# Loading the first weight matrix of a decode step in two transfers, 16 rows and 112 rows

## The chip, the core and the metric

One Trainium2 chip, one of its cores. The metric is the device time of one execution in microseconds; the figure of the kernel before is the median of three runs, 1299.67 us (1299.64 to 1299.94 us). Profiles show one execution each, and their time is compared with the median below.

## The reference

A decode step of two sequences with one token each (B = 2, D = 512): the normalized token attends over a key and value cache of 32 heads with 8192 positions of 128 numbers each, the attention's output goes through `wo`, and it is multiplied by a gate that a small MLP computes from the same token. Everything is float32.

```python
xn = layernorm(x)
q  = (xn @ wq) split in 32 heads of 128
s  = softmax(q . k_cache / sqrt(128)) . v_cache  @ wo      # k_cache, v_cache: 2 x 32 x 8192 x 128
g  = silu(gelu(layernorm(xn) @ w1 + b1) @ w2 + b2)         # w1: 512 x 1376, w2: 1376 x 512
out = x + s * g
```

The caches are 256 MB each (2 x 32 x 8192 x 128 numbers of 4 bytes, in MB of 2^20 bytes); the weights `w1`, `w2`, `wq` and `wo` are some 22 MB together.

## The kernel before, in words

The 64 pairs of sequence and head are handled two at a time, in 32 units. A unit's keys are 128 partitions with 64 KB each, 8 MB, and so are its values. Two buffers `kb` take the keys in turn, one buffer `vb` takes the values. For each unit VectorE multiplies the keys by the query (L550) and sums over the head's 128 numbers (L557), the maximum goes over TensorE (L564, L573), ScalarE takes exponentials (L578), and TensorE multiplies them with the values (L601).

Before the first unit a prologue computes the query and the gate. Its weights lie in the buffers of the main loop, which are still free then: `wq` in `kb[0]`, and `w1`, `w2`, `x`, `b1`, `b2` and all small work tiles side by side in `vb` (L281 ff., hence a profile names them all `vb`). The prologue runs: layernorm of x (L391 to L396), transposes (L403), x times `w1` (L439, with the bias in L441), gelu, times `w2` (L481), the gate (L488 to L497), the query (L510, L515, L521, L522). At the end `wo` is loaded into `vb` in five pieces and multiplied (L674, L683), the gate is applied (L691, L692), and the result is stored (L693).

All transfers are issued by one queue, SyncE's (SP), through the helper `load` (L325), in the order of the program; each has a semaphore of its own. The prologue's order is

```python
    load(w1_sb, w1.rearrange("(p c) f -> p c f", p=P), "w1", ["w1"])
    load(x_sb, x.rearrange("b s d -> (b s) d"), "x", ["x"])
    load(w2_sb, w2.rearrange("f n -> (f n)").rearrange("(p e) -> p e", p=P), "w2", ["w2"])
```

and after it `b1`, `b2`, `wq`, the first unit's keys in two halves (L357), the second unit's keys (`load_k(1)`, L527) and the first unit's values (`load_v(0)`, L533). The second unit's keys go into `kb[0]` and so wait until L510 has read `wq` from it; the first values go into `vb` and so wait until the prologue has read all that lies there. From then on each load waits only for the reads of what its buffer held.

A row of `w1` here is what one partition gets: four rows of the matrix in a piece, 4 x 1376 numbers, 22,016 bytes without a gap in memory. The class `Plan` collects every operation with what it reads and writes (the keys in the lists) and puts in the semaphore waits; the order on each engine is that of the program.

Of the kernel before, what the change touches and what calls it, by code (L numbers as in the profile page):

```python
# [20 lines left out]
class Plan:  # L21
# [18 lines left out]
    def op(self, eng, fn, r=(), w=(), over=(), it=None, loop=False, dma=None):  # L40


        o = Op()
        o.eng, o.fn, o.it, o.loop, o.dma, o.tell = eng, fn, it, loop, dma, False
        need = {}

        def after(d, war):
            if d.dma is None and dma is None and d.eng == eng and (eng == "pe" or war):
                return
            if d.dma is None:  # L50
                if need.get(d.eng) is None or need[d.eng].idx < d.idx:
                    need[d.eng] = d
            else:
                k = ("dma", d.dma)
                if need.get(k) is None or need[k].idx < d.idx:
                    need[k] = d

        for k in r:
            if k in self.writer:
                after(self.writer[k], False)  # L60
        for k in list(w) + list(over):
            if k in self.writer:
                after(self.writer[k], False)
            for d in self.readers.get(k, ()):
                after(d, True)
        clock = self.clock[eng]
        need = {k: d for k, d in need.items() if clock.get(k, 0) < d.idx}
        o.deps = [(k, d) for k, d in need.items()
                  if not any(e is not d and e.done.get(k, 0) >= d.idx for e in need.values())]
        for _, d in o.deps:  # L70
            for k, v in d.done.items():
                clock[k] = max(clock.get(k, 0), v)
        own = eng if dma is None else ("dma", dma)
        self.count[own] = o.idx = self.count.get(own, 0) + 1
        o.done = dict(clock)
        o.done[own] = o.idx
        for k in w:
            self.writer[k] = o
            self.readers[k] = []
        for k in r:  # L80
            if k not in w:
                self.readers.setdefault(k, []).append(o)
        self.ops.append(o)
# [91 lines left out]
def decode_kernel(nc, x, kc, vc, wq, wo, w1, b1, w2, b2, out):  # L175
    P = 128
# [32 lines left out]
    def pe(fn, r=(), w=(), it=None, loop=False):  # L209
        op("pe", fn, r, w, it=it, loop=loop)  # L210

    def dve(fn, r=(), w=(), it=None, loop=False):
        op("dve", fn, r, w, it=it, loop=loop)

    def act(fn, r=(), w=(), it=None, loop=False):
        op("act", fn, r, w, it=it, loop=loop)
# [55 lines left out]
    def take(name, p, n, base=0, at=None):  # L272

        if at is None:
            at = used[0]
            used[0] += n
            assert used[0] <= KP * DH
        boot.append(name)
        return vb[base:base + p, at:at + n]

    w1_sb = take("w1", P, ND * F).rearrange("p (c f) -> p c f", f=F)  # L281
# [18 lines left out]
    yT = take("yT", P, ND * B).rearrange("p (c b) -> p c b", b=B)  # L300
# [13 lines left out]
    def bank():  # L314
        i = turn[0] % 4
        turn[0] += 1
        return scratch[i], f"s{i}"
# [6 lines left out]
    def load(dst, src, sem, w, over=(), it=None):  # L324
        op("sp", lambda *i: nc.sync.dma_start(dst, src(*i) if callable(src) else src), (), w, over=over,  # L325
           it=it, loop=it is not None, dma=sem)
# [21 lines left out]
    WIDE = WO_PIECES[-4]  # L348


    load(w1_sb, w1.rearrange("(p c) f -> p c f", p=P), "w1", ["w1"])
    load(x_sb, x.rearrange("b s d -> (b s) d"), "x", ["x"])
    load(w2_sb, w2.rearrange("f n -> (f n)").rearrange("(p e) -> p e", p=P), "w2", ["w2"])
    for t, src, k in ((b1_sb, b1, "b1"), (b2_sb, b2, "b2")):
# [55 lines left out]
    for j in range(QT):  # L410
        pe(lambda j=j: matmul(px[R * j:R * j + RM, :P], pick, x_sb[:, j * P:(j + 1) * P],
                              start=True, stop=True), ["pick", "x"], [kx])
# [19 lines left out]
    def mlp():  # L432

        chunks = range(0, F, 512)
        for f in chunks:
            w = min(512, F - f)
            ph, k = bank()
            for c in range(ND):
                pe(lambda f=f, w=w, ph=ph, c=c: matmul(ph[:B, :w], yT[:, c, :], w1_sb[:, c, f:f + w],  # L439
                                                       start=(c == 0), stop=False), ["yT", "w1"], [k])  # L440
            pe(lambda f=f, w=w, ph=ph: matmul(ph[:B, :w], ones[R:R + 1, :B], b1_sb[:, f:f + w],  # L441
                                              start=False, stop=True), ["ones", "b1"], [k])
            act(lambda f=f, w=w, ph=ph: nc.scalar.copy(h_nat[:, 1 + f:1 + f + w], ph[:B, :w]),  # L443
                [k, "h_nat"], [("h_nat", f)])

        for m in range(QT):
            dve(lambda m=m: nc.vector.tensor_copy(  # L447
                h_row[:, :, m::QT],
                h_nat[:, WM * m:WM * m + WB * R].rearrange("b (k e) -> b e k", e=WB)[:, :WR, :]),
                ["h_nat"] + [("h_nat", f) for f in chunks], [("h_row", m)])  # L450
        ph, k = bank()
        for r in range(WR):
            pe(lambda r=r: transpose(ph[:, r * B:(r + 1) * B], h_row[:, r, :], ident[2 * R:2 * R + B, 2 * R:2 * R + B]),
               ["ident"] + [("h_row", m) for m in range(QT)], [k])

        act(lambda: nc.scalar.copy(h, ph[:, :WR * B].rearrange("p (r b) -> p r b", b=B)), [k], ["h"])
        dve(lambda: nc.vector.tensor_mul(u, h, h), ["h"], ["u"])
        dve(lambda: nc.vector.tensor_scalar(u, u, GELU_A, 1.0, op0=ALU.mult, op1=ALU.add), ["u"], ["u"])
        dve(lambda: nc.vector.tensor_mul(u, u, h), ["u", "h"], ["u"])
        act(lambda: nc.scalar.activation(u, u, AF.Tanh, scale=GELU_C), ["u"], ["u"])  # L460
        dve(lambda: nc.vector.scalar_tensor_tensor(u, u, 1.0, h, op0=ALU.add, op1=ALU.mult), ["u", "h"], ["u"])
        dve(lambda: nc.vector.tensor_scalar_mul(u, u, 0.5), ["u"], ["u"])

        parts = []
        for c in range(QT):
            for lo, hi, r, m in ((0, c + 1, 1, QT - 1 - c), (c + 1, QT, 0, 0)):
                if lo == hi:
                    continue
                parts.append(("hs", c, lo))

                def part(c=c, lo=lo, hi=hi, r=r, m=m):
                    shape = [P, WM, hi - lo, B]
                    return nc.vector.tensor_tensor(
                        out=hs[:, :, c, lo:hi, :], in0=u[:, r:r + WM, :].unsqueeze(2).to_broadcast(shape),
                        in1=cls[:, m:m + hi - lo].unsqueeze(1).unsqueeze(3).to_broadcast(shape), op=ALU.mult)
                dve(part, ["u"] + [("cls", m) for m in range(QT)], [parts[-1]])
        pw, kw = bank()
        for a in range(WM):
            j = a % QT
            w = min(512, WB * P - a * 512)  # L480
            pe(lambda a=a, j=j, w=w: matmul(pw[R * j:R * (j + 1), :w], hs[:, a].rearrange("p c j b -> p (c j b)"),  # L481
                                            w2_sb[:, a * 512:a * 512 + w], start=(a < QT), stop=(a + QT >= WM)),
               parts + ["w2"], [kw])
        act(lambda: nc.scalar.copy(g_sb, pw), [kw], ["g"])

        p, kp = bank()
        for c in range(QT):
            pe(lambda c=c: matmul(p[:, :P], fold[:, c, :], g_sb[:, c * P:(c + 1) * P], start=(c == 0), stop=False),  # L488
               ["fold", "g"], [kp])
        for j in range(QT):  # L490
            pe(lambda j=j: matmul(p[R * j:R * j + RM, :P], ones[R:R + 1, :], b2_sb[:, j * P:(j + 1) * P],
                                  start=False, stop=True), ["ones", "b2"], [kp])

        act(lambda: nc.scalar.copy(z, p[:, :P]), [kp], ["z"])
        act(lambda: nc.scalar.activation(th, z, AF.Tanh, scale=0.5), ["z"], ["th"])
        dve(lambda: nc.vector.scalar_tensor_tensor(th, th, 1.0, z, op0=ALU.add, op1=ALU.mult), ["th", "z"], ["th"])
        dve(lambda: nc.vector.tensor_scalar_mul(gate, th, 0.5), ["th"], ["gate"])  # L497

    mlp()

    for i in range(NQ):
        for c in range(ND):
            wv = wq_sb[:, c, :].rearrange("p (h s d) -> p h s d", s=U, d=DH)
            a = (NQ - 1 - i) * B
            for j in range(QT):
# [4 lines left out]
                    start=(i + c == 0), stop=(i == NQ - 1 and c == ND - 1)),  # L513
                   ["xnT"] + [("kb", 0, s) for s in range(2)], ["po"])
    act(lambda: nc.scalar.copy(q_nat, PO), ["po"], ["o4"])  # L515
    for k in range(N // NB):

        b, e = divmod(k, HH // NB)
        i, g = divmod(e, GQ)
        p, kp = bank()  # L520
# [147 lines left out]
    def piece(c):  # L668
        return ("wo", max(i for i, a in enumerate(WO_PIECES[:-1]) if a <= c))


    for c in range(WIDE):
        j = c % QT
        pe(lambda c=c, j=j: matmul(wide[R * j:R * j + RM, :], on[:, :, c], wo_sb[:, c, :],  # L674
                                   start=(c < QT), stop=(c + QT >= WIDE)), ["on", piece(c)], ["wide"])
# [47 lines left out]
```

## Time and profile before

| | |
|---|---|
| median of three runs | 1299.67 us (1299.64 to 1299.94) |
| the profiled execution's time | 1299.52 us |
| its span, first to last instruction | 1298.2 us |
| VectorE busy | 1134.3 us, 87% |
| TensorE busy | 408.3 us, 31% |
| ScalarE busy | 77.7 us, 6% |
| moved by DMA | 559.42 MB, mean 431 GB/s |
| w1 and w2, 2752 KB each | 9.3 and 15.0 us from issue to landing |
| mean granted TensorE clock | 0.629 |

A profile is read by its parts: busy time by engine, the span in 40 slices, the DMA queues, the chain of waits that ended last, and the groups of instructions. An engine's share of the span says little by itself; what counts is which wait ends last in each stage. "DMA share" is the mean share of time in which the core's 16 DMA engines were occupied by packets; since a packet is counted where it begins, short stretches show shares over 1. In the chain, a line that begins with DMA is time spent waiting for that transfer to land.

### The profile page before, as it was taken

The numbers are of one execution on the slowest core, as the hardware profiler recorded it, in microseconds if no ns is written. First come the engines' busy times: TensorE is split into PE (matmuls) and PEld (weight loads), VectorE is DVE, ScalarE is ACT, GpSimd is POOL, SyncE is SP. The second block draws the span as 40 slices with busy tenths as digits, with TensorE's granted clock in tenths as the row PEclk, the third lists the DMA queues.
The fourth block names the chain that finished last, engine by engine and source line by source line (L and its number), as shares of the span: only waits on it lengthen the run. The fifth ranks groups of instructions, "written<-read, shape, count | busy, mean of one in ns | idle before, by whom it ended". The sixth has DMA issues, their size and how long they took to land.

```text
span 1298.2 us, 6929 instructions
## 1 busy us (share of the span) xinstructions
PE 408.3 (31%) x2712; PEld 124.1 (10%) x2712; DVE 1134.3 (87%) x276; ACT 77.7 (6%) x250; POOL 2.6 (0%) x10
## 2 busy tenths in 40 slices
PE   5602333312333311333321333321333321333337
PEld 1200111000101000101100101100101100001102
DVE  2499999888889988889988888988888988888991
ACT  1200000000000000000000000000000000000000
POOL 0000000000000000000000000000000000000000
PEclk9856666556666556666555666655666655666659
DMA  9999999999999999999999999999999999999998
GB/s 404 447 422 445 428 420 446 426 444 428 436 432 424 446 426 442 428 426 444 424 446 426 436 432 424 446 426 442 428 428 442 424 446 426 438 430 424 433 434 363
DMA packets 10940, 559.42 MB, mean 431 GB/s; under 512 B 1220, under 2 KB 1332, under 8 KB 1592
## 3 DMA queue, kind: packets, MB, share of 16 engines
q1 hardware_dynamic: 10936, 559.36, 99.7%
q8 instruction: 3, 0.05, 0.0%
q14 instruction: 1, 0.01, 0.0%
HBM read 559.30 MB, written 0.06 MB: 431 GB/s over the span
## 4 chain that ended last, share of the span: by engine, by line
DMA 70%; PE 25%; DVE 3%; issue 1%; ACT 0%; SPq 0%; DVEq 0%
DMA vb<-in_A_v_cache_dram 67%; PE po L601 22%; DMA vb<-in_A_wo_dram 2%; DVE kb L550 1%; DVE sc L557 1%; PE s L439 1%; DMA vb<-in_A_x_dram 1%; PE po L510 1%; PE s L481 0%; PE s L441 0%; PE acc L683 0%; SPq L325 0%; DVE vb L447 0%; ACT L460 0%; PE s L488 0%
## 5 line engine op out<-in xcount | busy, mean ns | idle before, releaser
L550 DVE TENSOR_TENSOR kb<-kb,Q 128x8192 f32<-128x8192 f32 x64 | 555.5, 8681 | 102.7 <-DMA kb<-in_A_k_cache_dram 93.8
L557 DVE TENSOR_REDUCE sc<-kb 128x64 f32<-128x8192 f32 x64 | 552.3, 8666 | 0.0
L601 PE MATMUL po<-vb,PZ 128*8 128x512 f32 x1984 | 286.4, 742 | 288.2 <-DMA vb<-in_A_v_cache_dram 286.9
L573 PE MATMUL s<-nm,srow 1*128 1x2 f32 x64 | 18.4, 355 | 361.5 <-DVE nm L567 361.5
L601 PEld LDWEIGHTS po<-vb,PZ 128*8 128x8 f32 x1984 | 57.1, 104 | 491.3 <-issue 490.0
L564 PE MATMUL s<-ident,mx 128*1 128x128 f32 x32 | 11.8, 369 | 191.7 <-DVE mx L561 191.7
L573 PEld LDWEIGHTS s<-nm,srow 1*128 1x128 f32 x64 | 15.7, 303 | 370.8 <-DVE nm L567 370.8
L608 ACT COPY o<-po 128x512 f32<-128x512 f32 x32 | 18.7, 585 | 533.7 <-PE po L601 533.7
L574 ACT COPY bias<-s 128x2 f32<-128x2 f32 x32 | 5.1, 160 | 618.3 <-PE s L573 618.3
L610 PE MATMUL s<-mod,o 128*128 128x2 f32 x256 | 33.6, 253 | 22.1 <-ACT o L608 22.1
L610 PEld LDWEIGHTS s<-mod,o 128*128 128x128 f32 x256 | 31.0, 191 | 51.3 <-ACT o L608 51.3
L578 ACT ACTIVATE PZ<-sc,bias 64x128 f32<-64x128 f32 x64 | 25.5, 399 | 1.8
L564 PEld LDWEIGHTS s<-ident,mx 128*1 128x1 f32 x32 | 2.5, 79 | 195.1 <-DVE mx L561 164.7
L616 DVE TENSOR_TENSOR Z<-blk,s 128x8 f32 (+1 forms) x32 | 5.2, 163 | 12.4 <-PE s L610 12.4
L447 DVE COPY vb<-vb 2x384 f32<-2x384 f32 x4 | 1.8, 501 | 14.8 <-ACT vb L443 14.8
L578 ACT ACTIVATION_READ_ACCUMULATOR PZ<-sc,bias 64x1 f32 x64 | 11.8, 185 | 0.0
L691 DVE TENSOR_TENSOR gate<-acc,gate 128x128 f32<-128x128 f32 x1 | 0.3, 292 | 13.2 <-PE acc L683 13.2
L439 PE MATMUL s<-vb 128*2 128x512 f32 (+1 forms) x24 | 11.4, 623 | 0.3 <-ACT vb L404 0.3
L561 DVE TENSOR_REDUCE mx<-sc 128x1 f32<-128x128 f32 x32 | 9.2, 286 | 1.1
L582 ACT ACTIVATE ZR<-half,rs 128x8 f32 (+1 forms) x32 | 9.6, 301 | 4.1
L601 PE MATMUL po<-kb,PZ 128*8 128x512 f32 x64 | 8.8, 710 | 1.4 <-ACT PZ L578 1.4
L567 DVE TENSOR_REDUCE nm<-s 1x2 f32<-1x128 f32 x32 | 8.7, 272 | 0.3 <-PE s L564 0.3
(89 smaller groups left out, 84.3 us busy)
## 6 DMA issues: line engine op xcount, KB each, us to landing
kb<-in_A_k_cache_dram SPq DMA_DIRECT2D x4, 4096.0 KB, 43.1
kb<-in_A_v_cache_dram SPq DMA_DIRECT2D x2, 4096.0 KB, 40.4
vb<-in_B_w_dram SPq DMA_DIRECT2D x2, 2752.0 KB, 12.2
vb<-in_A_wo_dram SPq DMA_DIRECT2D x1, 4096.0 KB, 19.7
vb<-in_A_wo_dram SPq DMA_DIRECT2D x1, 2048.0 KB, 24.5
vb<-in_A_wo_dram SPq DMA_DIRECT2D x1, 1280.0 KB, 27.1
vb<-in_A_wo_dram SPq DMA_DIRECT2D x1, 512.0 KB, 27.9
vb<-in_A_v_cache_dram SPq DMA_DIRECT2D x31, 29.1
```

The source lines that it names most:

```text
L439: pe(lambda f=f, w=w, ph=ph, c=c: matmul(ph[:B, :w], yT[:, c, :], w1_sb[:, c, f:f + w], start=(c == 0), stop=False), ["yT", "w1"], [k])
L510: pe(lambda i=i, c=c, wv=wv, a=a, j=j, hd=hd: matmul(PO[R * j:R * j + NQ * B, :].rearrange("m (h d) -> m h d", d=DH), xnT[:, c, a:a + NQ * ...
L550: vector(n, n, lambda n: nc.vector.tensor_tensor(out=k, in0=k, in1=cols(Q, n * DH, DH).unsqueeze(1).to_broadcast([P, M, DH]), op=ALU.mult) ...
L557: vector(n, n, lambda n: nc.vector.tensor_reduce(out=SC[:, s * M:(s + 1) * M], in_=k, axis=AX.X, op=ALU.add), [("kb", i, s)], [("sc", s)])
L561: vector(n, n, lambda n: nc.vector.tensor_reduce(out=MX, in_=SC, axis=AX.X, op=ALU.max), [("sc", 0), ("sc", 1)], ["mx"])
L564: pe(lambda i: transpose(PM[:1, :P], MX, ident), ["mx", "ident"], ["s1"], it=n, loop=n > 0)
L573: pe(lambda i: matmul(PN[:, :U], srow, NM, start=True, stop=True), ["srow", "nm"], ["s2"], **one)
L578: act(lambda i, r=r, s=s: nc.scalar.activation(PZ[r, :, s, :], sc[r], AF.Exp, bias=BIAS[r, s:s + 1], scale=SCALE, accum_out=RS[r]), ["bias ...
L582: act(lambda i: nc.scalar.activation(cols(ZR, i * UP - UP, UP), half, AF.Copy, scale=RS), ["half"] + [("rs", s) for s in range(U)], [("ZR" ...
L601: pe(lambda i, t=t, j=j, v=v: matmul(PO[R * j:R * j + U * JW, :], PZ[:, t].rearrange("p s j -> p (s j)"), v[:, t * JW:(t + 1) * JW, :].rea ...
L608: act(lambda i: nc.scalar.copy(O4, PO), ["po"], ["o4"], **one)
L610: pe(lambda i, k=k: matmul(PT[:, :U], O4[:, k * DH:(k + 1) * DH], mod[:, k:U * JW:JW], start=(k == 0), stop=(k == JW - 1)), ["o4", "mod"], ...
```

## The change

`w1` is loaded in two transfers: the rows of partitions 0 to 15 first, then those of partitions 16 to 127. Each has its own semaphore, and the product with `w1` waits for both. Addresses, row lengths and all other transfers are the same.

```diff
-    load(w1_sb, w1.rearrange("(p c) f -> p c f", p=P), "w1", ["w1"])
+    w1_r = w1.rearrange("(p c) f -> p c f", p=P)
+    for a, e in ((0, 16), (16, P)):
+        load(w1_sb[a:e], w1_r[a:e], f"w1{a}", [("w1", a)])
     load(x_sb, x.rearrange("b s d -> (b s) d"), "x", ["x"])
...
                 pe(lambda f=f, w=w, ph=ph, c=c: matmul(ph[:B, :w], yT[:, c, :], w1_sb[:, c, f:f + w],
-                                                       start=(c == 0), stop=False), ["yT", "w1"], [k])
+                                                       start=(c == 0), stop=False), ["yT", ("w1", 0), ("w1", 16)], [k])
```

In the order of instructions this adds one transfer to SP's queue, ahead of all others, and a second semaphore to the wait of the first L439. Nothing else moves on any engine; the lines behind the change have numbers higher by two.

## The prediction

> **What bounds the kernel now.** I read the page first: its DMA rows in 40 slices, the queues, and the chain that ended last.
>
> ```profile
> span 1298.2 us, 6929 instructions
> DMA  9999999999999999999999999999999999999998
> q1 hardware_dynamic: 10936, 559.36, 99.7%
> DMA 70%; PE 25%; DVE 3%; issue 1%; ACT 0%; SPq 0%; DVEq 0%
> ```
>
> One hardware queue moves 559.36 MB and keeps the 16 DMA engines occupied for 99.7% of the span; only the last slice falls below 9 tenths. VectorE is busy for 87%, but transfers hold 70% of the chain. Next I cut the span into stages.
>
> ```profile
> core 0: us, PE busy (x) PEld busy (x) DVE busy (x) ACT busy (x) POOL busy (x), PEclk, DMA share, GB/s
> 0.00:2.00 2.00, 0.00 (x0) 0.00 (x0) 0.65 (x10) 1.26 (x1) 1.23 (x8) 1.00 0.67 154
> 2.00:10.00 8.00, 0.43 (x8) 0.10 (x8) 3.05 (x7) 0.23 (x2) 1.36 (x3) 1.00 0.92 394
> 10.00:36.00 26.00, 16.90 (x58) 4.35 (x58) 7.18 (x31) 4.30 (x11) 0.00 (x0) 0.92 0.99 428
> 46.00:56.00 10.00, 9.29 (x43) 3.49 (x36) 4.54 (x1) 4.18 (x8) 0.00 (x0) 1.00 1.00 433
> 133.00:1261.00 1128.00, 331.47 (x2199) 99.23 (x2203) 1032.66 (x206) 58.80 (x203) 0.00 (x0) 0.61 1.00 433
> 1294.00:1298.20 4.20, 1.87 (x60) 1.02 (x48) 0.58 (x2) 0.00 (x0) 0.00 (x0) 1.00 0.09 28
> ```
>
> The last two columns matter. From the first load to 1294 us the engines hardly rest: share 0.99 to 1.00, and 433 GB/s through the 1128 us of the main loop, so 27.1 GB/s per engine. There is no idle stretch in which an early loss could be made up: a microsecond that every engine loses in the first load is a microsecond at the end. Last, the two ends of the chain of waits:
>
> ```profile
> 0.75 0.39 SPq L325
> 1.20 8.32 DMA vb<-in_A_x_dram
> 9.57 0.65 PE s L411 x8
> 14.92 5.25 PE s L439 x8
> 41.92 7.02 PE po L510 x64
> ...
> 1266.48 27.11 DMA vb<-in_A_wo_dram
> 1293.59 0.04 issue
> 1293.63 2.29 PE acc L683 x64
> 1295.94 0.30 DVE gate L691
> 1296.27 0.29 DVE gate L692
> ```
>
> x is 4 KB and still takes 8.32 us: issued behind w1, it waits until w1's rows have left its engines, so each engine serves its rows in order of issue. At the other end wo is queued at 1266.5 us and lands at 1293.6 us, and 4.6 us of fixed work follow. The end is thus the end of the stream plus a constant.
>
> The execution took 1299.52 us, 1.32 us beyond its span of 1298.2 us; the median of the runs is 1299.67 us, 0.15 us more. I add my sum to the 1299.52 us and then those 0.15 us. A measurement of this kernel can tell about 0.2%, or 2.6 us, from no change.
>
> **The change part by part.** What it removes is one transfer of 128 rows; what it adds is one of 16 rows, one of 112, one issue on SP's queue, and a second flag for PE's L439.
>
> The issue, with the rows of SP's queue and of the tile of w1 and w2:
>
> ```profile
> 0.75 0.39 SPq L325 DMA_DIRECT2D vb<-in_B_w_dram  x1
> 1.58 0.35 SPq L325 DMA_DIRECT2D vb<-in_B_w_dram  x1
> 2.68 0.35 SPq L325 DMA_DIRECT2D kb<-in_A_wq_dram  x1
> 3.08 46.21 SPq L325 DMA_DIRECT2D kb<-in_A_k_cache_dram  x3
> 56.83 0.33 SPq L325 DMA_DIRECT2D vb<-in_A_v_cache_dram  x1
> ...
> L325 SPq DMA_DIRECT2D vb<-in_B_w_dram x2: 351/372/393, 0.8 to 1.6; - x2
> DMA to landing us min/median/max: 9.3/12.2/15.0
> ```
>
> An issue holds SP for 0.33 to 0.39 us, so x, w2, b1, b2, wq and the first two halves of K are issued some 0.4 us later. All of them queue behind w1, whose rows occupy the engines until about 10 us (0.75 + 9.3); the issues are over by about 4 us. The cost is nothing under that cover, and 0.4 us without it.
>
> The start. By 10 us the engines have moved 154 x 2 + 394 x 8 us = 3.46 MB, which at 433 GB/s takes 8.0 us: 2.0 us are lost at the start, 1.14 us of them before the first issue has ended (0.75 + 0.39). A first transfer of 16 rows can be cut into pieces sooner, but at most the other 0.9 us can be won. Bounds 0 and -0.9 us; I take 0, since one issue of either kind comes first.
>
> The pace of a row. w1 lands at 0.75 + 9.3 = 10.05 us and w2 at 1.58 + 15.0 = 16.58 us: 6.5 us for w2's 128 rows, eight to an engine, so 0.82 us per row of 22 KB. The loop's 27.1 GB/s gives 0.81 us. I call 0.82 us a row-time. In sum each engine still has eight row-times of w1, one in the first transfer and seven in the second. If every row keeps its pace, the split costs nothing.
>
> Does it? No row here shows a large transfer on part of the partitions: all that keep full pace span 128. So I bound it. Suppose that the partitions reach the memory by 16 paths, one row at a time each, and that 128 rows use them evenly: eight partitions to a path, an own path for every engine, which is what full pace with 16 engines looks like. Then 16 neighbouring partitions lie on 16 paths at best (s = 1 row to a path) and on two at worst (s = 8). With s rows to a path the first transfer takes s row-times and the paths it does not touch stand idle. Those still have all their eight rows of w1 to take, so w1 ends after s + 8 row-times and not 8: a floor of s x 0.82 us, which is +1.6 us for s = 2, +3.3 us for s = 4, +6.5 us for s = 8, and 0 for s = 1. I take s = 4, the middle of the end prices, 0 and 6.5 us. To the floor comes that blocks of seven rows do not fall on paths of eight evenly: engines meet on a path now and then while another is free. Bounds 0 and, with every second row met, three row-times, 2.5 us; I take one row-time, 0.8 us, as engines on a path where nobody meets them run ahead into w2. Sum: 3.3 + 0.8 = 4.1 us.
>
> [...]
>
> The flag. L439 waits for both parts of w1 and for yT, and all of PE's queue stands behind it. In the chain above it starts 5.35 us after x has come (14.92 against 9.57). x stands behind both parts on its engines, so by the time yT is there w1 is too, unless some engine ends w1 over 5 us after those that carry x. Cost 0, with under 0.1 us for the wait itself.
>
> The chain behind x. x comes later by what its engines lose, up to 5.8 us with both terms at their ends, and L439 and L510 with it. L510's end releases the third K transfer, issued at 49.3 us (3.08 + 46.21). Until then the stream lives on w1, w2, wq and the first K: 2752 + 2752 + 8192 + 8192 KB = 22.4 MB, 51.8 us at 433 GB/s, from 2.0 us on, so to 54 us. The reserve is 4.5 us, less about 1 us from issue to first bytes; and the stream itself ends later by at least the first transfer's extra 2.5 us, so 6 us in all. The next release, V at 56.8 us, comes while K streams for 19 us. The delay stays covered, and the 4.1 us are not doubled.
>
> Forecast: 1299.52 + 4.1 + 0.15 = 1303.8 us. Its own range goes from the floor less the best start, 3.3 - 0.9 = +2.4 us, to 3.3 + 2.5 = +5.8 us: 1302.1 to 1305.5 us.
>
> **The rivals.**
> *Every row keeps its pace, and the start is earlier* (not slower). Place: the first load. The engine itself is the limit, at 27.1 GB/s, whatever partition it writes; then 1 + 7 row-times are 8, and sooner pieces win 0 to 0.9 us: 1298.8 to 1299.7 us, about 1299.4 us. For it: engines at one steady pace in all stages, which an engine's own limit would give as well. Against it: nothing, except that 128 rows never put two engines on one path and so can't tell. It decides where s is 1. A variant is that the change does not do what it says: were the 16 rows taken by the engines that had them before, several to one, each engine's eight rows would be the same, and so would the time, 1299.7 us.
>
> *Two rows to a path*: +1.6 us plus up to 0.8 us, 1301.3 to 1302.1 us, slower but within 0.2%.
>
> *Neighbouring rows meet in the second transfer as well.* If rows are dealt to the engines in turn, as cards are, each of the eight rounds has 16 neighbours: 8 x 3 row-times with s = 4, +19.6 us, 1319 us. Against it: the 128-row loads are handed out in a way that avoids just that.
>
> *The stream runs dry before K.* If x came over 6 us later than its engines' own loss explains, the third K would be late and every further microsecond idle for all: with 3 us more, 1306.8 us. Nothing speaks for it but the reserve of 4.5 us.
>
> **How the numbers follow.** The forecast has 0.72: only the assumption that paths bind is open, and with it all but the two smallest s lie beyond 2.6 us. Every row at its pace has 0.14, two rows to a path 0.06, dealing in turn 0.05, the dry stream 0.03. The forecast's own range ends just below 2.6 us, which costs it 0.03. Slower by over 0.2%: 0.72 - 0.03 + 0.05 + 0.03 = 0.77. Within 0.2%: 0.14 + 0.06 + 0.03 = 0.23, of which I leave 0.02 for faster, as the start can't win over 0.9 us. The range has to reach the rival of no cost, or more than 2 in 10 would be left out: 1299.2 to 1305.8 us; its own range for the forecast is given above.
>
> **What would show it.** Right: the first transfer of w1 takes 3 to 4 us where a row took under one; the stretch from 2 to 10 us carries clearly less than 394 GB/s, nearer 250; x lands 2 to 6 us later; w2 lands at 20 to 22 us and not at 16.6; the loop keeps 433 GB/s; wo lands and the span ends some 4 us later. Wrong: w2 at 16 to 17 us, 394 GB/s again and an unmoved end (paths don't bind); w2 beyond 30 us (dealing in turn); a DMA share below 0.9 between 46 and 60 us (the dry stream).

## The result, and the profile after

The changed kernel takes 1304.84 us, median of six runs (1304.57 to 1306.33), against 1299.66 us (1299.31 to 1299.94, six runs) of the kernel before: a ratio of 1.0041, with a 95% interval of 1.0028 to 1.0054. It is 5.2 us slower, where 4.1 us were forecast; 1303.8 us was predicted, with a range of 1299.2 to 1305.8 us and 0.77 for slower. The profiled execution took 1304.72 us, its span is 1303.4 us, 5.2 us more than before, and what lies around the span is the same 1.32 us.

The page of the kernel after, and the row of rates from the page before:

```profile
span 1303.4 us, 6930 instructions
DMA  9999999999999999999999999999999999999998
GB/s 334 449 420 443 424 442 426 440 426 440 428 426 442 422 446 422 444 424 444 424 442 426 440 426 442 424 440 428 428 440 422 446 422 444 424 442 426 429 433 362
DMA 70%; PE 25%; DVE 3%; issue 1%; ACT 0%; SPq 0%; DVEq 0%
```

```profile
GB/s 404 447 422 445 428 420 446 426 444 428 436 432 424 446 426 442 428 426 444 424 446 426 436 432 424 446 426 442 428 428 442 424 446 426 438 430 424 433 434 363
```

The DMA engines are as occupied as before, and the chain has the same shares. Only the rate of the first slice tells of it: 334 GB/s, and 404 before. That the row of occupied tenths says nothing is a reading to keep: a packet counts as busy time for as long as it takes, and from 2 to 10 us the share is 0.95 at 226 GB/s, where it was 0.92 at 394.

The windows of the start, first of the kernel after, then the two of the kernel before that were not shown yet (last columns: granted clock, DMA share, GB/s):

```profile
0.00:2.00 2.00, 0.00 (x0) 0.00 (x0) 0.65 (x10) 1.26 (x1) 1.23 (x8) 1.00 0.76 132
2.00:10.00 8.00, 0.00 (x0) 0.00 (x0) 2.60 (x6) 0.22 (x2) 1.35 (x3) 1.00 0.95 226
10.00:36.00 26.00, 16.12 (x46) 3.47 (x46) 4.75 (x17) 2.62 (x8) 0.00 (x0) 1.00 1.04 420
36.00:46.00 10.00, 5.61 (x34) 1.93 (x34) 2.88 (x15) 1.68 (x3) 0.00 (x0) 0.66 0.85 367
46.00:56.00 10.00, 8.60 (x82) 2.81 (x82) 0.52 (x2) 1.75 (x4) 0.00 (x0) 1.00 1.01 431
56.00:94.00 38.00, 7.38 (x17) 2.91 (x17) 36.20 (x6) 4.69 (x8) 0.00 (x0) 0.63 1.03 448
133.00:1261.00 1128.00, 327.93 (x2177) 98.86 (x2177) 1033.54 (x207) 60.28 (x209) 0.00 (x0) 0.60 1.00 433
```

```profile
36.00:46.00 10.00, 9.31 (x78) 3.01 (x74) 0.52 (x2) 1.16 (x3) 0.00 (x0) 0.86 1.06 457
56.00:94.00 38.00, 1.11 (x3) 0.08 (x1) 37.93 (x6) 1.09 (x2) 0.00 (x0) 0.54 1.02 440
```

From 2 to 10 us the rate is 226 GB/s and was 394, at a share of 0.95. Rate times width, summed from 0 to 94 us, gives 40.2 MB before and 38.0 MB after: 2.2 MB less, which at 433 GB/s is 5.1 us. So the whole difference is there by 94 us, and the main loop runs at 433 GB/s in both. (A packet counts where it begins, so a single stretch such as 36 to 46 us is not to be read by itself.)

The transfers of the start by size, and the two ends of the chain after:

```profile
vb<-in_B_w_dram SPq DMA_DIRECT2D x1, 2752.0 KB, 19.9
vb<-in_B_w_dram SPq DMA_DIRECT2D x1, 2408.0 KB, 14.2
vb<-in_B_w_dram SPq DMA_DIRECT2D x1, 344.0 KB, 5.1
```

```profile
1.66 13.46 DMA vb<-in_A_x_dram
...
1272.40 26.39 DMA vb<-in_A_wo_dram
1298.80 0.04 issue
1298.84 2.27 PE acc L685 x64
```

The first 344 KB land 5.1 us after their issue. x lands at 15.12 us (1.66 + 13.46), before at 9.52 us; w2, issued at 2.03 us, at 21.9 us, before at 16.58 us; wo at 1298.80 us, before at 1293.59 us. What is lost in the first 15 us arrives at the end unreduced.

### The profile page after: what moved, and what is told of

It reads as the page before. It is cut to its first block, busy times and chain, and to the rows that moved or that the text cites. A ratio compares the mean times of both kernels' runs of the same rounds, so it can differ in the third digit from the quotient of the medians.

```text
span 1303.4 us, 6930 instructions
## 1 busy us (share of the span) xinstructions
PE 410.7 (32%) x2712; PEld 124.3 (10%) x2712; DVE 1134.3 (87%) x276; ACT 77.7 (6%) x250; POOL 2.6 (0%) x10
## 4 chain that ended last, share of the span: by engine, by line
DMA 70%; PE 25%; DVE 3%; issue 1%; ACT 0%; SPq 0%; DVEq 0%
DMA vb<-in_A_v_cache_dram 67%; PE po L603 22%; DMA vb<-in_A_wo_dram 2%; DVE kb L552 1%; DVE sc L559 1%; DMA vb<-in_A_x_dram 1%; PE s L441 1%; PE po L512 1%; PE s L483 0%; PE s L443 0%; SPq L325 0%; PE acc L685 0%; DVE vb L449 0%; ACT L462 0%; PE s L490 0%
## 5 line engine op out<-in xcount | busy, mean ns | idle before, releaser
L441 PE MATMUL s<-vb 128*2 128x512 f32 (+1 forms) x24 | 11.8, 644 | 0.3 <-ACT vb L406 0.3
## 6 DMA issues: line engine op xcount, KB each, us to landing
vb<-in_B_w_dram SPq DMA_DIRECT2D x1, 2408.0 KB, 14.2
vb<-in_A_wo_dram SPq DMA_DIRECT2D x1, 512.0 KB, 27.1
```

## The experiments

Two theories stood against each other. The first (P, later M): the engines crowd on some of the ways into the memory, because 16 neighbouring partitions, or blocks of seven rows, don't spread as 128 rows do. The second (rival T, later H): any additional or small transfer at the head of the stream costs, wherever its rows lie.

**Two transfers, cut along the row.**

```diff
-    load(w1_sb, w1.rearrange("(p c) f -> p c f", p=P), "w1", ["w1"])
+    w1_f = w1.rearrange("(p c) f -> p (c f)", p=P)
+    w1_to = w1_sb.rearrange("p c f -> p (c f)")
+    for a, e in ((0, 688), (688, ND * F)):
+        load(w1_to[:, a:e], w1_f[:, a:e], f"w1{a}", [("w1", a)])
...
```

The dots stand for the line of the product, which waits for both parts as in the change; the diffs of the other cuts of `w1` below leave it out as well.

> The kernel before, with w1 in two transfers of the same sizes as in the change (344 KB ahead of 2408 KB), but cut along the row and not across the partitions: both transfers have 128 rows, of 2752 B and of 19,264 B. Theory P (paths: the time is lost because rows of few partitions, and blocks of seven rows, crowd on some paths into the memory while others idle): each engine keeps a path of its own, no loss, 1299.4 to 1300.0 us, perhaps up to 0.9 us better by an earlier start. Rival T (a second transfer at the head of the stream costs, wherever its rows lie): about 1304.8 us, as in the change.

Measured: 1299.26 us (1299.05 to 1299.52), the kernel before beside it 1299.63 us, ratio 0.9997 (0.9988 to 1.0006). Number of transfers, their sizes and their order are those of the change, and nothing is lost; the rival that any second transfer costs has fallen. The 0.4 us by which it is below the kernel before can't be told from nothing.

```profile
vb<-in_B_w_dram SPq DMA_DIRECT2D x1, 2752.0 KB, 14.1
vb<-in_B_w_dram SPq DMA_DIRECT2D x1, 2408.0 KB, 8.4
vb<-in_B_w_dram SPq DMA_DIRECT2D x1, 344.0 KB, 3.1
```

The same 344 KB land after 3.1 us and not 5.1, the same 2408 KB after 8.4 us and not 14.2.

**16 extra rows, in three places.** The next three kernels differ only in the partitions that 16 additional rows of 22 KB go to; all three read the same rows of `w1`.

```diff
+    load(kb[1][0:16, :ND * F], w1.rearrange("(p c) f -> p (c f)", p=P)[:16], "extra", [("kb", 1, s) for s in range(2)])
     load(w1_sb, w1.rearrange("(p c) f -> p c f", p=P), "w1", ["w1"])
# the second: kb[1][32:96:4, ...]; the third: kb[1][0:32:2, ...]; the rest of the line is the same
```

> The kernel before with one more load ahead of all others: 16 rows of w1, 22 KB each, into partitions 0 to 15 of a key buffer that is overwritten later; w1 itself stays one transfer of 128 rows, and the result is not changed. It measures the first term of the change by itself, with one more row per engine. Theory P with four rows to a path: four row-times of 0.82 us, +3.3 us, 1302.9 us. Theory P with two: +1.6 us, 1301.3 us. Without paths, bytes alone: +0.8 us, 1300.5 us. Rival T: about +5 us or more, and the same in the next two kernels.

> As the kernel with the extra load of 16 rows, but its rows go to every fourth partition from 32 to 92, so each of the 16 blocks of four neighbouring partitions between 32 and 95 gets one. Same bytes, same descriptors, same place in the queue. Theory P, if a path is a block of four neighbours and the block 32 further on (and the halves of 64 are apart): one row to a path, one row-time, +0.8 us, 1300.5 us. If paths are grouped in another way: up to +3.3 us. Rival T: the same as with partitions 0 to 15.

> As before, the 16 extra rows in every second partition from 0 to 30: two rows to each of eight blocks of four. Theory P with blocks of four: two row-times, +1.6 us, 1301.3 us, half way between the other two. Rival T: the same as with partitions 0 to 15.

Measured, beside the same 1299.63 us: partitions 0 to 15, 1301.93 us, +2.3 us (ratio 1.0018, 1.0009 to 1.0027); every fourth from 32 on, 1300.66 us, +1.0 us (1.0008, 0.9999 to 1.0017); every second from 0 on, 1300.99 us, +1.4 us (1.0011, 1.0002 to 1.0020). The order of the medians is that of theory P, but the distance between the ends is 1.3 us and not 2.5. The eleven times for partitions 0 to 15 (from 1301.71 us) lie above all times of the other two (up to 1301.11 us); those two overlap, and the interval of the +1.0 us includes no change. How the transfer itself fared stands in the tile's row of the time to landing; its first number is the extra transfer, for the three kernels in the order above:

```profile
DMA to landing us min/median/max: 5.0/11.0/16.8
```

```profile
DMA to landing us min/median/max: 3.2/9.5/15.0
```

```profile
DMA to landing us min/median/max: 4.0/9.7/15.3
```

With the blocks of four neighbours that the expectations assume, one row to a block lands after 3.2 us, two after 4.0, four after 5.0: +0.8 us, a row-time, for the second row, and +1.8 us for all three further rows, where three row-times are 2.5 us. In the second and the third kernel SP's first issue took 0.60 and 0.61 us and not 0.40, for a reason that stays open; that makes both some 0.2 us later, and the distance to the first by as much too small.

The extra load also holds back the first unit's keys, which go into the same buffer: with partitions 0 to 15 their issue waits until 5.81 us, where it stood at 3.08 us. The stream does not feel that, because `w1`, `w2` and `wq` are queued ahead, 14.0 MB or some 32 us at 433 GB/s. The same holds for the other extra loads below.

**The 112 rows by themselves.** As above, with the rows of partitions 16 to 127 as the extra load.

```diff
+    load(kb[1][16:128, :ND * F], w1.rearrange("(p c) f -> p (c f)", p=P)[16:128], "extra", [("kb", 1, s) for s in range(2)])
```

> The kernel before with one more load ahead of all others: the 112 rows of w1 for partitions 16 to 127, into a key buffer that is overwritten later; w1 itself stays one transfer of 128 rows, the result is not changed. It measures the second transfer of the change by itself. Each engine has seven rows more, 7 x 0.82 = 5.7 us. The 16 extra rows on partitions 0 to 15 cost 1.5 us beyond their bytes (2.3 - 0.8), so of the change's 5.2 us some 3.7 us are left for this transfer. Theory M (engines meet on paths because seven rows don't fit blocks of four): 5.7 + 3.7 = +9.4 us, 1309.1 us. Theory F (the 112 rows run at their own pace, all of the loss comes of the first transfer's idle paths): +5.7 us, 1305.4 us.

Measured: 1308.92 us beside 1299.42 us, +9.5 us (1.0072, 1.0055 to 1.0088), as theory M has it. The window that holds most of this transfer, and one of the same kernel behind it:

```profile
3.00:12.00 9.00, 0.00 (x0) 0.00 (x0) 1.61 (x6) 0.00 (x0) 0.43 (x1) 1.00 1.03 269
14.00:24.00 10.00, 1.55 (x15) 0.97 (x15) 3.83 (x14) 0.87 (x4) 0.00 (x0) 1.00 1.00 430
```

The transfer of 112 rows ran at 269 GB/s, the 128 rows behind it at 430; the share is 1.03 and 1.00. So most of the loss of the change is this one: beyond the time of their bytes the 112 rows cost 9.5 - 5.7 = 3.8 us and the 16 rows 2.3 - 0.8 = 1.5 us; together 5.3 us, where the change cost 5.2.

**The parts exchanged.**

```diff
-    for a, e in ((0, 16), (16, P)):
+    for a, e in ((0, 112), (112, P)):
```

> The change with its parts exchanged: w1 in 112 rows (partitions 0 to 111) and then 16 rows (112 to 127). Theory M: the 112 rows lose 3.7 us wherever they start; the 16 rows again lie four to a path, and without the start-up of the stream to cover part of it they cost up to 3 row-times, 2.5 us: +5.2 to +6.2 us, 1304.9 to 1305.9 us. Rival H (what costs is the small transfer at the head of the stream): about the kernel before, 1299.7 us.

Measured: 1305.07 us beside 1299.42 us, +5.7 us (1.0042, 1.0025 to 1.0059). That is inside theory M's range. With the 112 rows at the head of the stream the loss is not less than in the change. The rival that blamed the small transfer at the head has fallen by this as well.

**Two halves.**

```diff
-    for a, e in ((0, 16), (16, P)):
+    for a, e in ((0, 64), (64, P)):
```

> The change with another cut: w1 in 64 rows (partitions 0 to 63) and 64 rows (64 to 127), four rows for each engine in each. Theory M with paths of four neighbours and the four 32 further on: two engines on each of eight paths throughout both transfers, 16 row-times and not 8, +6.5 us less up to 1 us that the start-up covers: 1305.1 to 1306.1 us. If large transfers on half of the partitions kept the pace: 1299.7 us. If the loss grows with unequal sizes of the two parts: less than in the change.

Measured: 1306.79 us, +7.4 us beside the same 1299.42 us (1.0056, 1.0039 to 1.0072), 0.7 us above the upper end of the expectation. The rate in 40 slices of the first 70 us shows the mechanism best:

```profile
GB/s 0 302 201 201 201 239 201 214 204 352 440 415 705 150 599 599 300 300 599 524 75 599 599 225 375 449 449 374 487 328 524 374 506 374 580 318 599 524 112 562
```

Slices are 1.75 us. While the two halves of w1 come in, the rate falls to 201 GB/s, slightly under half of 433 (201 to 239 in the third to the ninth slice); from the eleventh slice on w2 follows with 128 rows, and it is 440 and 415. At 201 GB/s 2752 KB take 14.0 us, and at half of 433 they would take 13.0; that 1.0 us more covers the 0.7 us. (Later slices jump because rows of 64 KB are counted where they begin.)

**The same cut in wq,** whose rows are 64 KB, in the running stream.

```diff
-    load(wq_sb, wq.rearrange("(p c) n -> p c n", p=P), "wq", [("kb", 0, s) for s in range(2)])
+    wq_r = wq.rearrange("(p c) n -> p c n", p=P)
+    for a, e, s in ((0, 16, 0), (16, P, 1)):
+        load(wq_sb[a:e], wq_r[a:e], f"wq{a}", [("kb", 0, s)])
```

> The kernel before with wq, not w1, cut into 16 and 112 rows; its rows are 64 KB, three times as long, and it comes in the middle of the running stream. Theory M: the loss is in row-times, each now 2.42 us: 112 rows 3.7 / 0.82 = 4.5 row-times, 10.9 us, and 16 rows 1.8 to 3 row-times, 4.4 to 7.3 us: +15 to +18 us, 1315 to 1318 us. A fixed cost per added transfer, or one of the start: +5 us or nothing, 1299.7 to 1305 us.

Measured: 1320.63 us, +21.2 us (1.0164, 1.0147 to 1.0181). The loss grew from 5.2 us with rows of 22 KB to 21.2 us with rows of 64 KB, where a cost of a transfer or of the start would have stayed the same; but it is 3 to 6 us more than the expectation. The rate in 40 slices of the first 70 us, the landing of both transfers, and that of `wq` in the kernel before:

```profile
GB/s 0 365 403 415 415 418 440 491 729 151 0 0 0 412 187 0 449 150 0 562 37 524 75 524 75 374 187 75 412 150 131 150 412 393 487 384 393 487 393 487
```

```profile
L325 SPq DMA_DIRECT2D kb<-in_A_wq_dram x2: 315/368/420, 2.6 to 3.0; - x2
DMA to landing us min/median/max: 24.2/39.5/54.9
```

```profile
kb<-in_A_wq_dram SPq DMA_DIRECT2D x1, 33.3
```

Slices are 1.75 us again, and a row counts where it begins. In the three slices from 17.5 to 22.75 us no row begins on any engine, though at the loop's 27.1 GB/s for an engine a row of 64 KB takes 2.42 us: the 16 rows of the first transfer are all under way and slow. They land at 2.6 + 24.2 = 26.8 us, the others at 3.0 + 54.9 = 57.9 us; `wq` in one transfer landed at 2.68 + 33.3 = 36.0 us in the kernel before. That is 21.9 us later, and the end comes 21.2 us later. Ahead of `wq` stands `w2`, which landed at 16.58 us in the kernel before, so 128 rows in one transfer took 19.4 us from there, 8.0 row-times of 2.42 us for an average of eight rows to an engine. The 16 rows take 10.2 us from there, 4.2 row-times for one row; counted from `w2`'s landing in this kernel, 18.5 us (1.58 + 16.9), it is 3.4. The 112 rows take 31.1 us, 236 GB/s, 12.9 row-times for seven rows: 5.9 too many, where 3.8 / 0.82 = 4.6 were carried over from the extra load of 112 rows. Why blocks of seven longer rows lose more row-times is not settled.

**64 extra rows, in two places.** The last pair keeps number and size of the rows and moves the block: 64 neighbouring partitions, on average four rows to an engine, in both. They also read other rows of `w1`; with 16 rows above the place mattered although the rows read were the same.

```diff
+    load(kb[1][32:96, :ND * F], w1.rearrange("(p c) f -> p (c f)", p=P)[32:96], "extra", [("kb", 1, s) for s in range(2)])
# the other: 0:64 in both places
```

> The kernel before with an extra load of 64 rows of w1, 22 KB each, ahead of all others into partitions 32 to 95 of a key buffer that is overwritten later (result not changed). Four rows to each engine, and by theory M (a path is a block of four neighbours together with the block 32 further on, the halves of 64 apart) each engine's four rows are one whole block and all 16 paths are used: four row-times, +3.3 us, 1302.8 us. If any 64 partitions are half of the paths: as the next kernel.

> The same 64 extra rows into partitions 0 to 63. Theory M: each block and the one 32 further on share a path, so eight paths with two engines each; in the cut into halves a row took 1.70 us under that: 4 x 1.70 = +6.8 us less about 0.5 us of start-up: 1305.8 to 1306.3 us. If only the number of rows counts: +3.3 us, 1302.8 us, as with partitions 32 to 95.

Measured beside 1299.50 us: partitions 32 to 95, 1303.33 us, +3.8 us (1.0028, 1.0017 to 1.0040); partitions 0 to 63, 1306.92 us, +7.4 us (1.0055, 1.0039 to 1.0072). The windows, first of 32 to 95, then of 0 to 63:

```profile
3.00:6.50 3.50, 0.00 (x0) 0.00 (x0) 1.60 (x6) 0.00 (x0) 0.42 (x1) 1.00 0.91 390
```

```profile
3.00:10.00 7.00, 0.00 (x0) 0.00 (x0) 1.61 (x6) 0.00 (x0) 0.42 (x1) 1.00 0.97 201
```

390 against 201 GB/s, and 3.6 us between the two, for the same number of rows and bytes. In the terms of theory M, partitions 0 to 31 and 32 to 63 share their ways (201 GB/s), 32 to 63 and 64 to 95 do not (390 GB/s). Theory M stands. No view shows the ways, or which engine carries which row; that an engine takes neighbouring rows, and each engine as many as the others, is inferred from these rates.

## Why the prediction was right, and where its sum was not

The direction and the mechanism were right, and the size nearly: 4.1 us were forecast, 5.2 us came, and 1304.84 us lies in the range and in the forecast's own range of 1302.1 to 1305.5 us. But the two terms that make the sum were each off, in opposite directions. That the sum came within 1.1 us is in part luck, and so is s = 4, which no run had shown and which the prediction took as the middle between two end prices.

To compare the terms with the runs, the floor has to be shared out: of its four row-times three are the 16 rows' own beyond their bytes, 2.5 us, and the fourth, 0.8 us, falls to the 112 rows, because in the prediction's picture a path that the first transfer leaves out has eight rows to take where an engine has seven. The forecast thus had 2.5 us for the 16 rows and 0.8 + 0.8 = 1.6 us for the 112; the runs show 1.5 and 3.8 us.

- *The stream has no slack.* Right. x, w2 and wo all land 5.2 to 5.6 us later, and the span is 5.2 us longer.
- *The issue costs nothing.* Right: x is issued at 1.66 us and not at 1.20, and the cut along the row, with the same additional issue, loses nothing (1299.26 against 1299.63 us).
- *The start wins 0 to 0.9 us, taken as 0.* Not refuted: -0.4 us with the cut along the row, inside the interval. That 16 rows start sooner was not shown: the first packets begin between 1.7 and 1.8 us before and after.
- *Four rows to a path.* The choice was borne out: partitions 0 to 15, every second one, and every fourth one from 32 on rank as four, two and one row to a path do, with landings after 5.0, 4.0 and 3.2 us. The price was too high for this place: 2.5 us against 1.5. The sum charged the idle paths in full, as if all of them could have worked from the first microsecond. At the start they could not: even uncrowded, 344 KB needed 3.1 us from issue to landing, while crowded they needed 5.0, so 1.9 us were there to be lost. That the start covers the rest fits the cut of `wq`, where the 16 rows come in the running stream and take 2.4 to 3.2 row-times too many, while the extra load of 16 rows has 1.5 / 0.82 = 1.8. No experiment separated it.
- *Blocks of seven rows.* This step failed. It put the meetings at one row-time, 0.8 us, at most 2.5 us; with the floor's fourth row-time that is 1.6 us, at most 3.3. The 112 rows by themselves cost 3.8 us beyond their bytes: 269 GB/s, 1.6 row-times for every row. The loss does not come now and then, it lasts through the whole transfer: in slices of 1.75 us, the five from 3.5 to 12.25 us carry 264, 239, 277, 277 and 214 GB/s. The step counted paths and rows in the sum and did not lay out which engine's row is on which path at each turn.
- *The flag.* Right. L441 (L439 before) starts 5.35 us after x in both: 20.52 against 15.17 us.

The row of TensorE's timeline for that, and those of SP's queue for the next point:

```profile
15.17 0.60 PE L413 MATMUL s<-vb,pick 2*2 2x128 f32 x8 [15.17 <-DMA vb<-in_A_x_dram]
20.52 5.70 PE L441 MATMUL s<-vb 128*2 128x512 f32 x8 [0.35 <-ACT vb L406]
```

```profile
3.46 52.10 SPq L325 DMA_DIRECT2D kb<-in_A_k_cache_dram  x3
63.09 0.33 SPq L325 DMA_DIRECT2D vb<-in_A_v_cache_dram  x1
```

- *The chain behind x.* Right that it stays covered. The third K transfer is issued at 55.56 us (3.46 + 52.10) and not at 49.29, 6.3 us later, slightly over the 5.8 us allowed: x came 5.6 us later, and L441's first eight products took 5.70 us and not 5.25. The stream did not run dry, with 431 GB/s from 46 to 56 us and 448 from 56 to 94.

Of the rivals, "every row keeps its pace" was refuted by 269 and 201 GB/s against 444, 430 and 433 for 128 rows. Two rows to a path, as a reading of partitions 0 to 15, does not fit a landing of 5.0 us there against 4.0 us on every second partition. Dealing in turn was refuted by its own size, +19.6 us, and by the 390 GB/s of partitions 32 to 95. Of the signs that the prediction named, the 226 GB/s from 2 to 10 us, x 5.6 us later, `w2` at 21.9 us and the 433 GB/s of the loop came as said; the first transfer took 5.1 us to its landing, more than the 3 to 4 us named.

The row for the 444 GB/s, the kernel before from 3 to 10 us:

```profile
3.00:10.00 7.00, 0.43 (x8) 0.10 (x8) 2.05 (x7) 0.00 (x0) 0.42 (x1) 1.00 1.04 444
```

## What to carry to other kernels

Where the transfers bound the kernel, a load that has to be cut is cut along the row, with all 128 partitions in each piece: that cost nothing in the one such cut measured, while cuts across the partitions cost 5.2 to 7.4 us on 2752 KB and 21.2 us on 8192 KB. In this stream without idle time the loss at the start stayed until the end (5.1 us by 94 us, 5.2 us at the end), so the first load deserves the same care as the loop. And a full row of DMA occupancy is no proof of a full rate (here a share of 0.95 at 226 GB/s): read GB/s beside it.

## What was not expected of the hardware

- A transfer of 112 rows ran at 269 GB/s with rows of 22 KB and at 236 GB/s with rows of 64 KB, not much better than half of the partitions (201 GB/s), though it leaves out only an eighth of them.
- 64 neighbouring partitions can have nearly the full rate or half of it: 390 GB/s for 32 to 95, 201 GB/s for 0 to 63.
